# Two more groups of an attention and mixer kernel computed together with 7 block products instead of 8, and the attention of the last pairs placed earlier

## Chip, core and metric

One core of one Trainium2 chip runs the whole program. The time is device microseconds of one execution; runs of the same kernel agree within a few tenths of a per cent. Engines: PE (TensorE, matrix products), PEld (its weight loads), DVE (VectorE), ACT (ScalarE), POOL (GpSimd), SP (SyncE, which issues most transfers).

## What is computed

Batch 8, 8 heads, 576 rows, head width 64. Attention within chunks of 64 rows, then a low-rank mixing along the sequence, then a two-layer network on each row:

```python
scores = scale * np.matmul(q_c, k_c.transpose(0, 1, 2, 4, 3))   # 64 x 64 a chunk
attn = np.exp(scores - max); attn = attn / (sum + 1e-09)
x = np.matmul(attn, v_c)                        # to (8, 576, 512)
u = x + (xt @ U @ V).transpose(0, 2, 1)         # U: 576 x 32, V: 32 x 576
ch = np.maximum(u @ w_ch1, 0.0) @ w_ch2         # 512 -> 2048 -> 512
return u + ch
```

## The kernel before

**Tiles.** Two batches make a pair (pr 0 to 3) of 1152 rows, nine tiles of 128 rows (t 0 to 8). Three tiles are a group (pr, g). The network's 2048 inner columns are 16 blocks f of 128.

**Products in three parts.** Each float32 operand is split into a high part, rounded to fp32r, and a low part, the rest (ACT casts the high part, DVE or POOL subtracts it from the whole). A product is high x high, high x low and low x high.

**A plain block** (pr, g, f) is `hidden` (L1140): 12 products of 384 columns (4 of 128 inputs x 3 parts), relu on ACT (`relu_high`, tile hh) and its low part on DVE (`relu_low`, hl), and `project_out` (L1167): 3 tiles x 3 products of 512 columns. The second half of block f runs after the first half of block f+1, so its relu has time. Eight groups run like this: (0,0) to (2,1).

**A joint group** (`joint`, L1483) takes two groups at once, before ((2,2),(3,0)) and ((3,1),(3,2)). The products with w_ch1 of both groups are 2 x 2 blocks in which 7 block products take the place of 8, with sums of the operands (Strassen and Winograd's form). `combos` (L1348) makes the sums of the weights once (`wsum` on POOL and DVE, `wput` to DRAM, array wc); `Combos` (L1427) makes those of the inputs (`csum` on POOL, tiles us; `csplit`, high on ACT, low on DVE or POOL). A joint group has four chunks of four f. In a chunk the steps follow the list STEPS: A1 to A7 and B1 to B7 are block products, 6 products of 384 columns each, 84 in all, on the banks x, c and y of A and of B; Ga0 to Gb5 are the second layer, 6 products of 512 columns each, 72 in all. Several block products add to one bank, and the bank is copied by ACT (`snap`, L1505, tiles s1, s5, u2, u3) between two of them, so that the later product has to wait for the copy. DVE adds the copies, takes the low parts of relu and adds the output to the residual (xr) after each Gb.

Each block product reads a combined weight block of 128 KB from wc into one of 11 places (`issue`, kind w), splits it (`split_w`: ACT casts, POOL or DVE subtracts, 5 steps ahead), and is issued again 11 products later.

**Attention beside it.** Pair 0 runs first, in a planned opening part of about 100 us in which the weights are converted too. Tiles of pairs 1 to 3 come two at a time, in visits (`VISITS` and `visit`, L1599 to L1628). At a visit PE makes the scores of two tiles (sc) and the values (av) of the two tiles of the visit before; DVE takes the maximum and subtracts (8 steps), ACT takes exp (ex), DVE scales the values (x). In between, q and k come through a DRAM copy in another layout (`permute`) and are transposed on DVE (`turn`, L950); ex is summed and transposed on DVE (`turn_ex`) and goes to DRAM and back (`put_ex`, `get_ex`: exs, eT); v is loaded by POOL (`load_v`, vn). Then x is split (xh, xl), projected onto U (`project`, bank y), spilled (xd), fetched again, mixed (`Mix`: bank u, added to x), transposed on DVE, stored (ud) and sent through DRAM (xs, uf) to get features onto partitions.

**What sets the order.** Everything after the opening stands in an agenda: `at(key, s, ...)` puts work at tick s, counted in quarter blocks on PE (a block has 4 ticks, a joint chunk 32). A table TUNE shifts each key by some ticks and names the queue or engine of each transfer or subtraction (S, P, A). The kernel is issued in that order, each engine takes its instructions in order, and there is no other scheduler. All tiles of attention share nine slots of 2 KB a partition (tag slot); all banks of products come from eight.

Of the kernel before, what the change touches and what calls it, by code (L numbers as in the profile page):

```python
# [231 lines left out]
def kernel(  # L232
# [1396 lines left out]
    for i, (s, now) in enumerate(chain):  # L1629
# [10 lines left out]
        for z, a in enumerate(prev):  # L1640
# [4 lines left out]
            if a.pr > 1:  # L1645
                at("spill " + a.n, s + 2 + z, a.spill)
# [117 lines left out]
```

## Time and profile before

| | us |
|---|---|
| median of 3 runs (all) | 920.66 (917.64, 920.66, 922.95) |
| profiled execution, own time | 916.5 |
| its span, first to last instruction | 914.7 |
| PE busy | 893.9 (98%) |
| DVE busy | 527.5 (58%) |
| ACT busy | 294.0 (32%) |
| POOL busy | 245.7 (27%) |
| share of PE in the chain that ended last | 80% |

A product is pipelined: the next one starts before it ends, so the time of one (338 ns for 384 columns) is longer than the step from one to the next, and a busy PE is not yet PE at its pace. The pace is read from stretches in which nothing waits. An idle engine costs nothing as long as PE doesn't wait for it.

### The profile page before, as it was taken

Reading aid. Unit: us, or ns where it says so; the run is one execution under the profiler, and the core shown is the slowest. Engines: PE = TensorE matmul, PEld = TensorE weight load, DVE = VectorE, ACT = ScalarE, POOL = GpSimd, SP = SyncE. Lnnn points to the kernel's source line nnn. Section 1 sums busy time; section 2 is a strip of 40 time slices with the busy share of each in tenths; the row PEclk is TensorE's granted clock in tenths of the full one; section 3 lists DMA queues with packets and bytes.
Section 4 is the critical chain, followed back from the end, with each engine's and each line's share of the span. In section 5 each row is a group of like instructions: output and inputs, shape, how many; then the busy total and the mean of one; then the engine's idle time right before and its main releaser. Section 6 shows DMA issues by size and latency. Waiting matters only on the chain.

```text
span 914.7 us, 17206 instructions
## 1 busy us (share of the span) xinstructions
PE 893.9 (98%) x6500; PEld 789.5 (86%) x6500; DVE 527.5 (58%) x1022; ACT 294.0 (32%) x602; POOL 245.7 (27%) x363
## 2 busy tenths in 40 slices
PE   6899999999999999999999999999999999999998
PEld 5578989888889889888888888898889889988996
DVE  4799995566544437556356646555745547534433
ACT  5576761122211112122112212212544326423430
POOL 4300001031020022232303212377643346323320
PEclk9999999999999999999999999999999999999999
DMA  9994695677557546667868677588554542522201
GB/s 183 195 323 138 157 231 107 134 166 186 92 129 156 97 109 136 162 164 136 199 147 198 154 182 183 149 213 276 167 195 119 150 146 58 196 64 64 81 18 69
DMA packets 298882, 137.91 MB, mean 151 GB/s; under 512 B 197424, under 2 KB 278224, under 8 KB 298800
## 3 DMA queue, kind: packets, MB, share of 16 engines
q1 hardware_dynamic: 200224, 109.29, 44.6%
q10 hardware_dynamic: 92640, 14.09, 9.2%
q0 software_dynamic: 5936, 13.43, 5.6%
q8 instruction: 51, 0.84, 0.4%
q14 instruction: 31, 0.25, 0.1%
HBM read 97.17 MB, written 53.74 MB: 165 GB/s over the span
## 4 chain that ended last, share of the span: by engine, by line
PE 80%; DVE 6%; DMA 6%; issue 2%; SPq 2%; POOL 2%; ACT 1%; ACTq 0%; DVEq 0%; POOLq 0%
PE o L1179 24%; PE h L1151 24%; PE o L1553 15%; DMA qkv<-in_q_dram 2%; PE sc L970 2%; SPq L284 1%; PE av L1028 1%; PE x_3B L1578 1%; PE x_0B L1578 1%; PE x_2B L1578 1%; DVE wraw L323 1%; PE x_1B L1578 1%; PE x_3A L1578 1%; PE x_2A L1578 1%; DVE wroom L326 1%
## 5 line engine op out<-in xcount | busy, mean ns | idle before, releaser
L1151 PE MATMUL h<-uth,w 128*128 128x384 f32 x1024 | 282.2, 338 | 0.4 <-DVE ex L985 0.4
L1179 PE MATMUL o<-w,hh 128*128 128x512 f32 x768 | 242.7, 397 | 0.1
L1151 PEld LDWEIGHTS h<-uth,w 128*128 128x128 f32 x1024 | 187.5, 188 | 6.9 <-issue 1.2
L1164 DVE SCALAR_TENSOR_TENSOR hl<-h,hh 128x384 fp32r<-128x384 f32 x128 | 70.5, 552 | 179.8 <-ACT hh L1159 179.5
L1151 PE MATMUL h<-utl,w 128*128 128x384 f32 x512 | 173.0, 338 | 0.0
L1159 ACT ACTIVATE hh<-h 128x384 fp32r<-128x384 f32 x128 | 62.7, 490 | 325.1 <-PE h L1151 317.1
L1179 PEld LDWEIGHTS o<-w,hh 128*128 128x128 f32 x768 | 141.7, 188 | 24.9 <-ACT hh L1159 0.7
L1179 PE MATMUL o<-w,hl 128*128 128x512 f32 x384 | 151.9, 396 | 1.2 <-DVE hl L1164 1.2
L284 POOL DMA_DIRECT2D vn<-in_v_dram x96 | 58.9, 628 | 232.7 <-issue 104.7
L1151 PEld LDWEIGHTS h<-utl,w 128*128 128x128 f32 x512 | 96.2, 188 | 5.1 <-issue 0.2
L1179 PEld LDWEIGHTS o<-w,hl 128*128 128x128 f32 x384 | 72.2, 188 | 19.7 <-DVE hl L1164 2.7
L1421 POOL TENSOR_TENSOR w<-w,w 128x256 fp32r<-128x256 f32 x65 | 49.5, 776 | 79.8 <-ACT w L1420 78.7
L1563 DVE TENSOR_TENSOR xr<-o,xr 128x512 f32<-128x512 f32 x48 | 32.9, 690 | 57.8 <-PE o L1553 57.6
L1420 ACT CAST w<-w 128x256 fp32r<-128x256 f32 x112 | 41.5, 408 | 24.2 <-DMA w<-wc 16.3
L1056 POOL TENSOR_TENSOR xl<-x,xh 128x512 fp32r<-128x512 f32 x8 | 10.3, 1289 | 137.7 <-ACT xh L1052 137.7
L1421 POOL TENSOR_TENSOR w<-w 128x256 fp32r<-128x256 f32 x35 | 26.5, 762 | 54.2 <-ACT w L1420 51.7
L993 ACT ACTIVATE ex<-ex 128x512 f32<-128x512 f32 x27 | 17.1, 633 | 66.4 <-DVE ex L985 52.4
L984 DVE TENSOR_REDUCE mx<-sc 128x4 f32<-128x256 f32 x54 | 22.5, 416 | 15.9 <-PE sc L970 15.9
L985 DVE TENSOR_TENSOR ex<-sc,mx 128x256 f32<-128x256 f32 x54 | 22.9, 424 | 2.3
L950 DVE STREAM_TRANSPOSE qn<-qn 128x512 f32<-128x512 f32 x27 | 18.8, 697 | 6.1 <-DMA qn<-qblocks 5.1
L313 ACT ACTIVATE wroom<-wraw 128x1024 f32<-128x1024 f32 (+1 forms) x19 | 19.0, 1001 | 5.5 <-issue 4.1
L1028 PE MATMUL av<-vn,eT 64*64 64x64 f32 x864 | 18.3, 221 | 2.3 <-DVE hl L1164 1.2
(345 smaller groups left out, 1428.3 us busy)
## 6 DMA issues: line engine op xcount, KB each, us to landing
wraw<-in_moe_w_ch_dram SPq DMA_DIRECT2D x32, 512.0 KB, 6.2
w<-wc SPq DMA_DIRECT2D x105, 128.0 KB, 2.3
xs<-xb SPq DMA_DIRECT2D x108, 64.0 KB, 2.2
uf<-xs SPq DMA_DIRECT2D x26, 256.0 KB, 3.2
qn<-qblocks SPq DMA_DIRECT2D x24, 256.0 KB, 3.7
kn<-kblocks SPq DMA_DIRECT2D x24, 256.0 KB, 4.2
vn<-in_v_dram POOLq DMA_DIRECT2D x96, 64.0 KB, 3.3
exs<-ex SPq DMA_DIRECT2D x96, 64.0 KB, 2.3
```

Source lines behind the costliest of these rows:

```text
L284: {"S": nc.sync, "P": nc.gpsimd, "A": nc.scalar}[way].dma_start(dst, src)
L985: nc.vector.tensor_sub(self.ex[:, e].rearrange("p b h k -> p h b k"), self.sc[e].rearrange("p (h b k) -> p h b k", b=2, k=TB), mx[:, e].un ...
L1028: nc.tensor.matmul(ps[e][cs, (z * HP + hp) * C : (z * HP + hp + 1) * C], lhsT=self.eT[rows, hp, 2 * c : 2 * c + 2, :].rearrange("p a i -> ...
L1151: nc.tensor.matmul(ps[:, :GN], lhsT=w[:, z, cc], rhs=u[:, cc, :], start=(n == 0), stop=(n == 3 * NCC - 1))
L1159: nc.scalar.activation(hh, ps[:, :GN], AF.Relu)
L1164: nc.vector.scalar_tensor_tensor(hl, ps[:, :GN], 0.0, hh, op0=ALU.max, op1=ALU.subtract)
L1179: nc.tensor.matmul(acc[j], lhsT=h[:, js], rhs=w2[f][:, z], start=(first and i == 0), stop=(final and i == 2),)
L1420: nc.scalar.copy(h, l.bitcast(F32))
L1421: side("wlo", n).tensor_sub(l, l.bitcast(F32), h)
L1553: nc.tensor.matmul(acc[j], lhsT=u[:, q, js], rhs=w2[f][:, p], start=(z == "A" and e == 0 and n == 0), stop=(z == "B" and e == 1 and n == 2),)
L1563: nc.vector.tensor_add(xs[j], acc[j], xs[j])
L1578: nc.tensor.matmul(ps, lhsT=w[wz][:, cc], rhs=u[uz][:, cc], start=(k in (1, 2, 5) and cc == 0 and m == 0), stop=(cc == 1 and m == 2), skip ...
```

## The change

A third joint group ((2,0),(2,1)) is put ahead of the two, so the joint part begins after (1,2), at tick 384 instead of 512. The plain blocks of (2,0) and (2,1) go. Attention of pairs 2 and 3 is placed at earlier ticks (pair 2 every 20 ticks, where it was 28 and more); since three tiles of pair 3 would come too late for that, four visits lie inside the first joint group. Tiles 6 to 8 of pair 1 are spilled and fetched as well, the mixes of pair 2 store their result for the residual, and the order table is new: nearly all of its shifts and many of its queues differ, of which a few lines stand here. Line numbers after the table are 35 higher.

```diff
-        "perm 3.0.3": "P", "perm 3.1.0": "A", "perm 3.1.2": "S", "perm 3.1.3": "A",
+        "perm 3.1.0": "P", "perm 3.1.2": "S", "perm 3.1.3": "A", "perm 3.1.4": "S", "put": "S",
-    JOINED = 8 * NF * 4
+    JOINED = 6 * NF * 4
-    JOINT = [((2, 2), (3, 0)), ((3, 1), (3, 2))]
+    JOINT = [((2, 0), (2, 1)), ((2, 2), (3, 0)), ((3, 1), (3, 2))]
     def free(f):
-        return ("hidden", 2, 1, f) in done and ("sum", f // 2) in done
+        return ("hidden", 1, 2, f) in done and ("sum", f // 2) in done
     VISITS = [
         (94, 1, 0), (114, 1, 2), (138, 1, 4), (158, 1, 6), (198, 1, 8),
-        (221.5, 2, 0), (262, 2, 2), (290, 2, 4), (318, 2, 6), (346, 2, 8),
-        (366, 3, 0), (394, 3, 2), (420, 3, 4), (446, 3, 6), (480, 3, 8),
+        (221.5, 2, 0), (242, 2, 2), (262, 2, 4), (282, 2, 6), (302, 2, 8),
+        (322, 3, 0), (344, 3, 2), (404, 3, 4), (428, 3, 6), (450, 3, 8),
     ]
-    chain.append((510, []))
+    chain.append((470, []))
-            if a.pr > 1:
+            if a.pr > 1 or a.t > 5:
                 at("spill " + a.n, s + 2 + z, a.spill)
-            s1 = s + 2 if after - s < 30 else s + 20
+            s1 = s + 2 if after - s < 30 or s == 344 else s + 20
-    for (pr, e), s in {(2, 0): 140, (2, 1): 196, (3, 0): 290, (3, 1): 340}.items():
+    for (pr, e), s in {(2, 0): 140, (2, 1): 184, (3, 0): 236, (3, 1): 330}.items():
+            at(f"fetch 1.{t}", PAIR + NF * 4 + 4 + 8 * (t - 6), lambda t=t: Mix(1, t).fetch())
-    for t in range(6):
-        at(f"fetch 2.{t}", (345, 408)[t > 2] + 3 * (t % 3), lambda t=t: Mix(2, t).fetch())
-        plan_mix(2, t, (350, 413)[t > 2] + 3 * (t % 3))
     MIXES = {
-        (2, 6): 392, (2, 7): 395, (2, 8): 398,
-        (3, 0): 462, (3, 1): 465, (3, 2): 468, (3, 3): 560,
+        (2, 0): 294, (2, 1): 297, (2, 2): 300, (2, 3): 332,
+        (2, 4): 335, (2, 5): 338, (2, 6): 410, (2, 7): 413, (2, 8): 416,
+        (3, 0): 438, (3, 1): 441, (3, 2): 444, (3, 3): 560,
-    for pr, g in ((0, 2), (1, 0), (1, 1), (1, 2), (2, 0), (2, 1)):
+    for pr, g in ((0, 2), (1, 0), (1, 1), (1, 2)):
         for f in range(NF):
```

How the order moves at three places. First PE in the second chunk of the first joint group, from the second-layer step Ga0 (tile o_1_0) on, in the kernel before:

```order
L1553 MATMUL o_1_0_7749<-w_1128,hh_1A 128x512 x2
L1553 MATMUL o_1_0_7749<-w_1128,hl_1A 128x512
L1553 MATMUL o_1_0_7749<-w_1160,hh_1A 128x512 x2
L1553 MATMUL o_1_0_7749<-w_1160,hl_1A 128x512
L1578 MATMUL x_1B<-w_1396,w_1306 128x384
L1578 MATMUL x_1B<-w_1454,w_1306 128x384
L1578 MATMUL x_1B<-w_1396,w_1353 128x384
```

and in the change:

```order
L1588 MATMUL o_1_0_6536<-w_1160,hh_1A 128x512 x2
L1588 MATMUL o_1_0_6536<-w_1160,hl_1A 128x512
L1005 MATMUL sc<-kn_6_6257,qn_6_6256 64x64 x16
L1005 MATMUL sc<-kn_7_6411,qn_7_6410 64x64 x16
L1063 MATMUL av<-vn_4_6330,eT_4_6364 64x64 x16
L1063 MATMUL av<-vn_5_6350,eT_5_6464 64x64 x16
L1613 MATMUL x_1B<-w_1396,w_1306 128x384
L1613 MATMUL x_1B<-w_1454,w_1306 128x384
L1613 MATMUL x_1B<-w_1396,w_1353 128x384
```

A visit (scores of tiles 3_6 and 3_7, values of 3_4 and 3_5) now stands between Ga0 and the block product B7 on bank x of B. As before, Ga1 and then B4, on the same bank, follow B7.

Second ACT at the same place: hh is relu, u_0_1B the copy of bank x_1B, ex an exp, xh a split of x, the CASTs of w are weight blocks. Before:

```order
L1519 ACTIVATE hh_1B<-y_1B 128x384
L1420 CAST w_1607<-w_1607 128x256
L1519 ACTIVATE hh_1B<-c_1B 128x384
L1507 COPY u_0_1B<-x_1B 128x384
L1420 CAST w_1649<-w_1649 128x256
L1519 ACTIVATE hh_1B<-u_0_1B 128x384
```

In the change:

```order
L319 DMA w_1259<-wc_5523 128x256
L1554 ACTIVATE hh_1B<-c_1B 128x384
L1028 ACTIVATE ex_6_6579<-ex_6_6579 128x512
L1028 ACTIVATE ex_7_6583<-ex_7_6583 128x512
L1542 COPY u_0_1B<-x_1B 128x384
L1455 CAST w_1661<-w_1661 128x256
L1087 CAST xh_4_6652<-x_4_6627 128x512
L1554 ACTIVATE hh_1B<-u_0_1B 128x384
```

Both exps of the visit now stand ahead of the copy of x_1B.

Third DVE at the end of the last plain group, where the inputs' sums are split for the first joint group (w_1160 is the low part for the products A2 and B2, bank y; w_951 that for A1). Before:

```order
L1164 SCALAR_TENSOR_TENSOR hl_1_15_7231<-h_1_15_7216,hh_1_15_7229 128x384
L1473 TENSOR_TENSOR w_1082<-us_2_7233,w_1021 128x4x2x32
L1473 TENSOR_TENSOR w_1160<-uf_8_7154,w_1128 128x4x2x32
L1473 TENSOR_TENSOR w_1259<-us_2_7233,w_1219 128x4x2x32
L1473 TENSOR_TENSOR w_1353<-us_2_7233,w_1306 128x4x2x32
L1473 TENSOR_TENSOR w_1454<-us_2_7233,w_1396 128x4x2x32
L1040 TENSOR_TENSOR x_8_7273<-av,sm_8_6937 128x256 x2
L1473 TENSOR_TENSOR w_1160<-uf_7_7147,w_1128 128x4x2x32
```

In the change:

```order
L1508 TENSOR_TENSOR w_1353<-us_1_5817,w_1306 128x4x2x32
L1508 TENSOR_TENSOR w_1160<-uf_2_5753,w_1128 128x4x2x32
L1199 SCALAR_TENSOR_TENSOR hl_2_15_5844<-h_2_15_5829,hh_2_15_5842 128x384
L1508 TENSOR_TENSOR w_1454<-us_1_5817,w_1396 128x4x2x32
L1508 TENSOR_TENSOR w_951<-uf_2_5753,w_614 128x4x2x32
L1508 TENSOR_TENSOR w_1082<-us_2_5863,w_1021 128x4x2x32
L1508 TENSOR_TENSOR w_1259<-us_2_5863,w_1219 128x4x2x32
```

The last split for bank y stood after the last block's low part of relu (hl_1_15), four other splits and a visit's scaling (x_8); it now stands ahead of that low part (hl_2_15), and no visit's steps are near.

## Rows read from the trace of the kernel before

**Rows 1.** The page: busy us (share) xinstructions; the span in 40 slices, tenths.

```profile
PE 893.9 (98%) x6500; PEld 789.5 (86%) x6500; DVE 527.5 (58%) x1022; ACT 294.0 (32%) x602; POOL 245.7 (27%) x363
PE   6899999999999999999999999999999999999998
PEclk9999999999999999999999999999999999999999
```

**Rows 2.** The chain that ended last, in order of time: start us, us, what.

```profile
340.26 2.11 PE h L1151 x12
342.38 2.09 PE o L1179 x9
865.76 13.94 PE o L1553 x60
```

**Rows 3.** Two windows: us, busy us (xinstructions) of each engine, clock, DMA share, GB/s.

```profile
340.26:352.89 12.63, 12.63 (x65) 11.44 (x64) 6.64 (x14) 2.50 (x5) 6.32 (x10) 1.00 0.68 140
834.41:865.76 31.35, 31.35 (x157) 28.20 (x157) 12.53 (x21) 10.93 (x28) 8.06 (x12) 1.00 0.16 47
```

**Rows 4.** Waits of PE, 100 to 914 us: us in total, times, longest us.

```profile
PE y_0A L1578 <- ACT w L1472: 1.3, 1, 1.3
PE av L1028 <- DVE hl L1164: 1.2, 1, 1.2
PE av L1028 <- DMA eT<-exs: 1.0, 2, 0.6
PE o L1179 <- DVE hl L1164: 0.9, 1, 0.9
PE h L1151 <- DVE ex L985: 0.4, 1, 0.4
PE y_0A L1578 <- DVE w L1473: 0.2, 1, 0.2
```

**Rows 5.** Timeline, one visit: start us, us, engine line op tiles [idle before <-releaser].

```profile
576.46 1.16 PE L970 MATMUL sc<-kn,qn 64*64 64x64 f32 x64
578.63 0.73 PE L1179 MATMUL o<-w,hh 128*128 128x512 f32 x2
580.20 0.63 ACT L993 ACTIVATE ex<-ex 128x512 f32<-128x512 f32 x1 [4.53 <-DVE ex L985]
580.99 0.63 ACT L993 ACTIVATE ex<-ex 128x512 f32<-128x512 f32 x1 [0.16 <-DVE ex L985]
```

**Rows 6.** Lines L1473 and L1507: count, duration ns min/median/max, first and last start.

```profile
L1473 DVE TENSOR_TENSOR w<-us,w x23: 407/650/982, 644.2 to 784.3; 128x256 fp32r<-128x256 f32 x23
L1473 DVE TENSOR_TENSOR w<-uf,w x18: 407/414/956, 648.0 to 785.2; 128x256 fp32r<-128x256 f32 x18
L1507 ACT COPY u_1B<-x_1B x4: 470/479/480, 702.2 to 832.0; 128x384 f32<-128x384 f32 x4
```

**Rows 7.** Two more windows, columns as in rows 3.

```profile
100.00:125.00 25.00, 25.00 (x127) 22.53 (x126) 24.37 (x30) 18.05 (x24) 0.00 (x0) 1.00 0.81 196
600.00:625.00 25.00, 23.80 (x206) 21.18 (x205) 15.36 (x32) 4.48 (x10) 14.34 (x21) 1.00 0.84 221
```

**Rows 8.** Timeline of PE at the start of the joint part.

```profile
658.95 0.41 PE L1578 MATMUL y_0A<-w 128*128 128x384 f32 x1 [1.30 <-ACT w L1472]
659.52 0.62 PE L1578 MATMUL y_0A<-w,w 128*128 128x384 f32 x2 [0.16 <-DVE w L1473]
```

**Rows 9.** The page's transfers (KB, us to landing); POOL's groups (busy us, mean ns).

```profile
w<-wc SPq DMA_DIRECT2D x105, 128.0 KB, 2.3
vn<-in_v_dram POOLq DMA_DIRECT2D x96, 64.0 KB, 3.3
L284 POOL DMA_DIRECT2D vn<-in_v_dram x96 | 58.9, 628 | 232.7 <-issue 104.7 <-DMA xs<-xb 38.8 <-DVE utl L1138 29.7
L1421 POOL TENSOR_TENSOR w<-w,w 128x256 fp32r<-128x256 f32 x65 | 49.5, 776 | 79.8 <-ACT w L1420 78.7 <-PE x_1B L1578 1.0
```

**Rows 10.** Timeline of SP's issues, 648 to 655 us.

```profile
649.33 3.46 SPq L284 DMA_DIRECT2D w<-wc  x6
```

439 rows, old and new, of the table TUNE are left out of this document.

## Prediction

> **What bounds the kernel now.** I began with the page: how busy each engine is and the course over the span [rows 1]. TensorE (PE) is busy 98% of 914.7 us at the full granted clock, VectorE (DVE) 58%, GpSimd (POOL) 27%. Since the end of a pipelined product is modelled, that share alone proves nothing, so I took the pace from the chain that ended last [rows 2] and from two clean windows [rows 3]. Twelve 384-wide products take 2.11 us and nine 512-wide ones 2.09; three blocks (a block is one f of one group of three tiles) take 12.63 us, 4.21 each, with no idle time on PE. A joint chunk of 84 narrow and 72 wide products takes 31.35 us, also without idle time. In the first window DVE is busy 6.64 of 12.63 us and in the second 12.53 of 31.35. Next come PE's own waits from 100 us on [rows 4]: they sum to 5.0 us out of 815. So PE's stream of products sets the end; all else matters only where PE is made to wait. The time before 100 us stays: on PE the two orders read alike until about there.
>
> The sum is made against the profiled execution: span 914.7, own time 916.5, which is 4.2 under the median of 920.66 (runs 917.64 to 922.95). I carry the difference over to the median.
>
> **The products.** Groups (2,0) and (2,1) cost 32 blocks, 32 x 4.21 = 134.7 us, and become four joint chunks, 4 x 31.35 = 125.4: **9.3 us less** [rows 3]. The count gives a little less: 384 narrow products become 336, the 288 wide ones stay, and 48 x 2.11/12 is 8.4 [rows 2]. The chunk also shows narrow products at a slightly better pace, (31.35 - 72 x 13.94/60)/84 = 0.174 us against 0.176, so I take **-9.0**, ends -8.4 and -9.3. The Trainium skill, "TensorE: Matmul & The Clock Gate", section "Back-to-back issue gap", gives N/2.4 + 2.5 ns a product at the full clock, 162.5 ns for 384 columns; by that estimate the term would be -7.8 and my sum below -4.9. The trace's 0.174 to 0.176 decides.
>
> **What is added off PE** is hidden unless PE waits for it. The orders count DVE 1024 to 1071 instructions, ACT 666 to 774, POOL 368 to 456, SP 692 to 751. In it are 56 more weight blocks (each a 128 KB load landing in 2.3 us [rows 9], an ACT cast, and a subtraction of 0.78 us on POOL [rows 9] or a shorter one on DVE), 18 more additions of output, 21 more splits and 12 more sums of the operands. With 84 product steps in hand this costs nothing by itself; if its cover goes, it is the third rival.
>
> **Where PE can be made to wait anew.** Before, no attention ran beside a joint group but the last mixes. Now three visits (scores of two tiles, values of the two before) and a fourth for values lie inside the first joint group. A joint chunk leaves DVE 31.35 - 12.53 = 18.8 us [rows 3]. The second chunk gets, by the order, six input transposes, eight softmax steps, four scalings, two tiles' row sums and transposes of ex, a split and eleven steps of mixing: about 20.5 us by their lengths (0.4 to 0.7 us each). DVE then works some 33 of about 36 us. It can be that full without harm: from 100 to 125 us it is busy 24.37 of 25 and PE loses nothing [rows 7]. But joint steps read DVE and ACT results sooner than plain blocks do.
>
> - *Second chunk, the step after the visit.* A visit of the trace [rows 5]: scores start at 576.46; PE is back at its products at 578.63 (2.17 later); ACT starts the two exps at 580.20 and 580.99, the second ends at 581.62 (5.16 later). Now ACT has both exps ahead of the copy of x_1B (shown in the order above), and PE's last product on that bank, B4, must wait for the copy. From the visit's start PE has 2.17, then B7 6 x 0.174 and Ga1 6 x 0.232: B4 is wanted at 4.61. The copy ends at 5.16 + 0.48 [rows 6] + 0.1 for the signals, about 5.7. Wait **1.1 us**, plus what DVE is late with the softmax; I take +1.5, ends 0 and 3.0. The projection of tile 3_5 then needs a split that stands behind nine DVE steps: +0.5, ends 0 and 1.0.
> - *First chunk.* On POOL the four transfers of vn_3_2 stand behind two weight subtractions: 2 x 0.78 + 4 x 0.63 to issue + 3.3 to land = 7.4 us [rows 9], where PE has B7, Ga1, B4, Gb0, Gb1 and the scores left, about 7.3. +0.6, ends 0 and 1.8. The split for tile 3_3 is as tight: +0.3, ends 0 and 0.6.
> - *Third chunk.* SP has 43 issues there and 49 in the second (before: 24 and 29), up to 0.58 us each [rows 10]; the values' eT may land late: +0.5, ends 0 and 1.5, by the waits on eT of before, 1.0 us over two visits [rows 4].
> - *Earlier visits* come about every 25 us where it was 33 to 40. The waits at values were 1.2 + 1.0 us [rows 4]; +0.5, ends -1.0 and 2.2.
> - *Start of the joint part.* PE waited 1.3 + 0.2 us for y_0A [rows 4, 8]: the last split for that product stood on DVE behind five others and a visit's scaling. Now it stands before the last block's split (order above), and no visit is near: **-1.0**, ends -1.5 and +1.5.
>
> Sum: -9.0 + 1.5 + 0.5 + 0.6 + 0.3 + 0.5 + 0.5 - 1.0 = **-6.1 us**: span 908.6, own time 910.4, median **914.6**. All lower ends give -11.8, all upper ones +3.2; they won't come together.
>
> **Rivals.**
> 1. *The new waits don't come* (the order leaves room everywhere). Then -9.0 - 1.0 = -10.0: **910.7**. For it: DVE at 97% cost PE nothing [rows 7]. Against: the B4 wait follows from lengths alone.
> 2. *The waits pile up.* DVE steps that read two operands from SBUF stretch while POOL works: one form of L1473 has a median of 0.414 us and a maximum of 0.956, the other, made beside POOL's sums, a median of 0.650 [rows 6]. POOL gets more work, and the order puts 14 such DVE steps into the first two chunks. At 0.24 to 0.54 us more each (0.650 and 0.956 less 0.41), DVE falls 3.4 to 7.6 us behind, and each of three visits makes PE wait 2 us more: -6.1 + 6 = -0.1, **920.6**, no change. The Trainium skill, "GPSIMD Engine Reference", section "1. Specifications", says that POOL shares its SBUF interfaces with VectorE and contends with DVE instructions of two SBUF inputs; by that rule, which the spread just named agrees with, this rival would be the outcome. Against it: most of DVE's added steps read PSUM or one operand, and my lengths already contain a mean of it.
> 3. *Slower: weight blocks come late behind SP.* In three chunks SP carries 138 issues (before 81), and weight loads stand behind transfers that wait for DVE or for each other's landing. ACT casts in order, so a late load holds back the copies that PE needs, step after step. If each of the 42 products waits 0.35 us, that is 14.7: -6.1 + 14.7 = +8.6, **929.3**. It decides from about 0.25 us a product (10.5 us, +4.4). For it: the densest SP stretch of before, 600 to 625 us with DMA 84% busy, is one where PE lost 1.2 [rows 4, 7]. Against: no product of the joint groups of before waits for a load, and loads are issued eleven blocks ahead.
>
> That the change doesn't do what it says is no rival: the order on PE shows 48 narrow products fewer.
>
> **How the numbers follow.** About 0.5% (4.6 us) is what a measurement of this kernel can tell from no change. Forecast (-8.5 to -4.6): 0.45. Rival 1: 0.17. Rival 2 (-4.6 to +4.6): 0.25. Rival 3: 0.13. So faster 0.62, same 0.25, slower 0.13. The range goes from a little below rival 1, 910.0, to 922.0, past rival 2's centre; left out are rival 3, the upper part of rival 2 and a little below: about 2 in 10.
>
> **What would show it.** Right: the four chunks of the new joint group at 31.3 us plus projections, mixes and visits; PE's waits in the first joint group 2 to 5 us in all, the longest at x_1B of the second chunk behind an ACT copy; about no wait at y_0A; the last two joint groups as before. Wrong: waits of PE's weight products on casts of w in most steps (rival 3); waits of 2 us and more at each visit with DVE over 95% in the first two chunks (rival 2); no wait over 0.5 us there (rival 1); or new idle time before 450 us, which I put at half a microsecond.

## The result and the profile after

The change is **slower** by 1.4%: median 933.43 us (932.18 to 934.07, 4 runs) against 921.14 (917.64 to 922.95, 4 runs), ratio 1.0136 with a 95% interval of 1.0104 to 1.0169. Forecast were 914.6 us and a range of 910 to 922. Unaltered once more beside later experiments it gave 934.53, ratio 1.0164 (1.0142 to 1.0186). The profiled execution took 933.8 us, its span is 932.0 (before 914.7, forecast 908.6). The page after, its first part and its line of the clock, answers to [rows 1]:

```profile
PE 895.8 (96%) x6452; PEld 785.1 (84%) x6452; DVE 560.6 (60%) x1069; ACT 327.5 (35%) x705; POOL 313.5 (34%) x451
PEclk9999999999999999999999999999999999999999
```

PE carries out 48 products fewer and yet is busy 2 us longer; its weight loads, PEld, fell by 4.4. The reason is in the rows below. PE's waits after, from 100 us on (in total, times, longest), to be read against [rows 4]:

```profile
PE y L1105 <- DVE xl L1091: 4.0, 5, 1.9
PE y L1104 <- ACT xh L1087: 2.6, 2, 1.7
PE sc L1005 <- DVE x L1226: 2.0, 1, 2.0
PE x_1B L1613 <- ACT u_1B L1542: 1.9, 1, 1.9
PE x_3B L1613 <- ACT u_3B L1542: 1.5, 2, 1.3
PE x_2A L1613 <- ACT u_2A L1542: 1.4, 2, 0.7
PE av L1063 <- DMA eT<-exs: 1.4, 2, 0.9
PE h L1186 <- DVE ex L1020: 1.2, 2, 0.8
PE x_0A L1613 <- ACT w L1507: 1.1, 1, 1.1
```

With eight smaller groups they sum to 20.5 us in 28 waits, before to 5.0 in 7. By stretch, in windows of before (columns as in [rows 3]):

```profile
100.00:350.00 250.00, 248.36 (x1810) 221.84 (x1809) 148.24 (x286) 66.57 (x116) 32.32 (x50) 1.00 0.64 141
350.00:525.00 175.00, 174.00 (x1501) 155.04 (x1500) 100.88 (x219) 35.17 (x67) 41.41 (x60) 1.00 0.71 164
525.00:675.00 150.00, 147.34 (x1083) 131.93 (x1082) 86.01 (x170) 40.73 (x94) 71.24 (x94) 1.00 0.71 200
```

and of the change, with a chunk of the last joint group and three windows of 25 us behind:

```profile
100.00:350.00 250.00, 246.15 (x1912) 218.58 (x1911) 156.02 (x306) 69.53 (x119) 42.15 (x62) 1.00 0.71 155
350.00:525.00 175.00, 165.51 (x1315) 145.50 (x1314) 98.74 (x205) 36.34 (x78) 90.31 (x119) 0.98 0.86 217
525.00:675.00 150.00, 142.78 (x1029) 123.32 (x1028) 103.71 (x192) 62.05 (x160) 79.13 (x111) 0.99 0.64 175
865.46:896.82 31.36, 31.36 (x158) 28.20 (x156) 12.17 (x21) 11.35 (x29) 8.84 (x12) 1.00 0.20 59
350.00:375.00 25.00, 22.82 (x220) 19.84 (x219) 15.11 (x34) 4.89 (x9) 7.85 (x12) 0.93 0.98 232
425.00:450.00 25.00, 23.09 (x192) 19.87 (x192) 13.13 (x27) 3.53 (x7) 9.01 (x12) 0.93 0.67 173
575.00:600.00 25.00, 22.85 (x215) 19.10 (x214) 21.40 (x44) 8.13 (x20) 12.10 (x18) 0.93 0.75 207
```

Length less PE's busy time is idle time. From 100 to 350 us it rose from 1.6 to 3.9, from 350 to 525 (plain blocks, visits of pairs 2 and 3) from 1.0 to 9.5, from 525 to 675 (the new joint group) from 2.7 to 7.2: **15.3 us more**. The chunk of the last joint group is as it was, 31.36 us, and 48 products are gone, so I count the products' 9.0 as given; in the new joint group no chunk is free of waits. And in three windows the granted clock is 0.93 where it was 1.00: 25 x 0.07 = 1.75 us of PE's work in each, **5.2 us**. That makes -9.0 + 15.3 + 5.2 = +11.5 of the 17.3 us of span, in this execution. The 5.2 need not be a cost by themselves: of the four executions one had a mean granted clock of 1.00, and its span was 931.3 us, 0.7 less than this one. Another part hides in the busy time: a product of PE is drawn with a modelled end, so a stop is longer than its idle time. At the wait of 1.87 us shown further down, the starts lie 2.27 apart where the pace is 0.23, so 2.04 are lost: 0.17 more. For 21 more stops that is 3.6 us; 2.2 are left unexplained. The Trainium skill, "Perfetto Trace Analysis", section "Tensor Engine Instruction (MATMUL, LD_WEIGHTS)", says that PE's end times are estimated from the size of the instruction; here PE's busy time rose by 2.0 with less work.

Where the time is lost can be listed by place. "Lost" is the time from start to start of PE's products over their pace [rows 2] (for the 64-wide ones of a visit 0.018 us, from [rows 5]), summed over the place, the slow clock behind it included; it is good to a few tenths. "Again" is the second execution, of the unaltered change.

| us | what PE waits for | lost | again |
|---|---|---|---|
| 363 to 370 | scores of 2_4, 2_5: additions of output on DVE behind a late k; then slow clock (not again) | 4.3 | 1.3 |
| 389 to 395 | values: low part of relu on DVE (again: eT) | 0.8 | 1.1 |
| 427 to 438 | projection of 2_6: relu and xh on ACT behind a load of k; slow clock | 4.0 | 6.2 |
| 472 to 477 | a visit's scores and values | 1.2 | 1.5 |
| 480 to 490 | projections of 3_0, 3_1: xh, xl behind the next visit's steps; again: slow clock | 4.8 | 6.5 |
| 531 to 536 | product A7: splits of its inputs | 2.3 | 2.2 |
| 555 to 563 | projections of 3_2, 3_3: xl | 1.2 | 1.8 |
| 579 to 593 | B4 behind the copy of x_1B; slow clock (not again) | 4.4 | 4.3 |
| 609 to 618 | copies of x_2A behind an exp | 2.5 | 2.5 |
| 653 to 661 | copies of x_3B behind splits for the next joint group | 2.2 | 2.2 |

Ten places, 28 us in one execution and 30 in the other. In the kernel before the same windows lose some 4 us, half of that at the start of its joint part (659 us).

Two of them in the timeline. First PE, ACT and ACT's queue of transfers (ACTq) at 426 to 436 us; "qn" and "kn" are q and k of tile 3_1, whose load ACT issues:

```profile
431.71 0.34 PE L1186 MATMUL h<-uth,w 128*128 128x384 f32 x1
433.72 0.49 PE L1104 MATMUL y<-xh,ust 128*128 128x512 f32 x1 [1.68 <-ACT xh L1087]
435.58 1.05 PE L1214 MATMUL o<-w,hh 128*128 128x512 f32 x2
...
425.83 0.61 ACTq L319 DMA_DIRECT2D qn<-qblocks  x1
432.02 0.55 ACTq L319 DMA_DIRECT2D kn<-kblocks  x1
432.67 0.49 ACT L1194 ACTIVATE hh<-h 128x384 fp32r<-128x384 f32 x1 [6.37 <-PE h L1186]
433.06 1.13 ACT L1087 CAST xh<-x 128x512 fp32r<-128x512 f32 x2
```

The load of k is issued at 432.0 instead of 426.4. The chain of waits names the cause: the slot it goes to was an xb tile, whose transfer xs, issued at 426.3, had not landed.

```profile
426.29 5.64 DMA xs<-xb
```

ACT takes its work in order, so relu and xh stand behind the load, and PE has nothing for 1.7 us and then only one product for another 0.2. What follows stands in windows of 1 us: the granted clock falls to half, 1.2 GHz, between 435 and 436 us, some 1.6 us after PE came back, and PE is busy while it stays there.

```profile
432.00:433.00 1.00, 0.05 (x1) 0.00 (x0) 0.00 (x0) 0.33 (x1) 0.00 (x0) 1.00 0.01 2
435.00:436.00 1.00, 1.00 (x4) 0.75 (x3) 1.00 (x4) 0.00 (x0) 0.92 (x1) 0.67 0.11 24
436.00:437.00 1.00, 1.00 (x4) 0.80 (x3) 0.67 (x2) 0.00 (x0) 0.37 (x1) 0.50 0.67 136
439.00:440.00 1.00, 1.00 (x7) 1.00 (x6) 0.00 (x0) 0.00 (x0) 0.00 (x0) 1.00 0.79 139
```

Second the place that the prediction named, the second chunk behind the visit of 3_6 and 3_7, on PE, ACT, DVE and POOL:

```profile
583.16 0.40 PE L1588 MATMUL o<-w,hl_1A 128*128 128x512 f32 x1
585.43 2.23 PE L1613 MATMUL x_1B<-w,w 128*128 128x384 f32 x6 [1.87 <-ACT u_1B L1542]
...
583.65 1.36 ACT L1028 ACTIVATE ex<-ex 128x512 f32<-128x512 f32 x2 [3.05 <-DVE ex L1020]
584.92 0.46 ACT L1542 COPY u_1B<-x_1B 128x384 f32<-128x384 f32 x1
...
586.83 1.43 DVE L1034 TENSOR_SCALAR sm<-sm 128x8 f32<-128x8 f32 x1
...
586.92 1.30 POOL L1091 TENSOR_TENSOR xl<-x,xh 128x512 fp32r<-128x512 f32 x1
```

The copy stands behind both exps, as forecast; 1.87 us for 1.1 to 1.5, and then the six products of B4 take 2.23 us at the slow clock. In the second execution the wait is there again, and the clock of this stretch stays at 1.00:

```profile
PE x_1B L1613 <- ACT u_1B L1542: 2.0, 1, 2.0
...
575.00:600.00 25.00, 21.87 (x217) 18.05 (x216) 21.43 (x43) 9.36 (x23) 13.16 (x19) 1.00 0.76 202
```

The place loses as much (4.3 for 4.4 us): PE's idle time is 3.1 us for 2.2, with waits of 0.6 us for the visit's values and for xl. So what the slow clock takes, other waits can take in its stead.

### The profile page after: what moved, and what is told of

Its sections match the earlier page's. It is cut to its first block, busy times and chain, and to the rows that moved or that the text cites. A ratio compares the mean times of both kernels' runs of the same rounds, so it can differ in the third digit from the quotient of the medians.

```text
span 932.0 us, 17562 instructions
## 1 busy us (share of the span) xinstructions
PE 895.8 (96%) x6452; PEld 785.1 (84%) x6452; DVE 560.6 (60%) x1069; ACT 327.5 (35%) x705; POOL 313.5 (34%) x451
## 4 chain that ended last, share of the span: by engine, by line
PE 78%; DVE 7%; DMA 6%; SPq 3%; ACT 2%; issue 2%; POOL 2%; ACTq 0%; DVEq 0%; POOLq 0%
PE o L1588 19%; PE o L1214 19%; PE h L1186 18%; DMA qkv<-in_q_dram 2%; SPq L319 2%; PE x_0A L1613 1%; PE x_2B L1613 1%; PE x_3A L1613 1%; PE x_3B L1613 1%; PE sc L1005 1%; PE x_1B L1613 1%; PE x_0B L1613 1%; DMA kn<-kblocks 1%; PE x_2A L1613 1%; PE x_1A L1613 1%
## 5 line engine op out<-in xcount | busy, mean ns | idle before, releaser
L1186 PE MATMUL h<-uth,w 128*128 128x384 f32 x768 | 211.6, 339 | 1.2 <-DVE ex L1020 1.2
L1214 PE MATMUL o<-w,hh 128*128 128x512 f32 x576 | 183.3, 399 | 0.5 <-ACT hh L1194 0.5
L1186 PEld LDWEIGHTS h<-uth,w 128*128 128x128 f32 x768 | 140.9, 188 | 6.0 <-issue 1.4
L1186 PE MATMUL h<-utl,w 128*128 128x384 f32 x384 | 130.0, 338 | 0.0
L1214 PEld LDWEIGHTS o<-w,hh 128*128 128x128 f32 x576 | 106.9, 189 | 19.7 <-ACT hh L1194 1.4
L1214 PE MATMUL o<-w,hl 128*128 128x512 f32 x288 | 114.9, 399 | 1.1 <-DVE hl L1199 1.1
L1456 POOL TENSOR_TENSOR w<-w,w 128x256 fp32r<-128x256 f32 x100 | 75.0, 761 | 118.4 <-ACT w L1455 117.3
L1186 PEld LDWEIGHTS h<-utl,w 128*128 128x128 f32 x384 | 72.3, 188 | 4.1 <-DVE utl L1173 0.4
L1588 PE MATMUL o<-w,hh_1B 128*128 128x512 f32 x72 | 23.1, 402 | 0.0
L1588 PE MATMUL o<-w,hh_2A 128*128 128x512 f32 x72 | 22.6, 395 | 0.0
```

The source lines that it names most:

```text
L1186: nc.tensor.matmul(ps[:, :GN], lhsT=w[:, z, cc], rhs=u[:, cc, :], start=(n == 0), stop=(n == 3 * NCC - 1))
L1214: nc.tensor.matmul(acc[j], lhsT=h[:, js], rhs=w2[f][:, z], start=(first and i == 0), stop=(final and i == 2),)
L1456: side("wlo", n).tensor_sub(l, l.bitcast(F32), h)
L1588: nc.tensor.matmul(acc[j], lhsT=u[:, q, js], rhs=w2[f][:, p], start=(z == "A" and e == 0 and n == 0), stop=(z == "B" and e == 1 and n == 2),)
```

## Experiments

Two theories to begin with. **A**: each place is one instruction that stands ahead of what PE needs, on an engine that works in order; mend the place and its time is saved. **B**: the transfers as a whole run short (the DMA engines are busy 0.86 from 350 to 525 us, before 0.71), so a mended place shows up elsewhere. The kernel before, measured beside each of them, took 918.5 to 920.3 us.

**One place each.** The numbers are shifts in the order table (quarter blocks) and queues; of each line of the table only the entries that change are shown.

```diff
-        "qk 3_1": "A"
+        "qk 3_1": "S"
```

> The changed kernel with one edit: the q and k of tile 3_1 are loaded by SP instead of ACT. In the changed kernel's trace the load of k stands on ACT from 425.8 to 432.0 us, waiting until a transfer of the input transposes has left the slot, and the relu behind it is 4 us late; PE waits 1.9 and 0.6 us for the projection of tile 2_6 at 431.7 and then runs at half the clock for some 3 us. Theory A (single instructions that stand ahead on an engine that works in order): all of it goes, 4.2 us less than the changed kernel, 929.2 for 933.4; no wait at that projection, no fall of the clock near 435. Theory B (the transfers are too slow as a whole, 0.86 of the DMA engines' time from 400 to 525 us): SP is held instead, what stands behind it comes late, and PE waits nearly as long a little later: 1 us less or none.

930.58 us, ratio 1.0107 (1.0076 to 1.0138). Theory A at its place: no wait, no idle time, full clock.

```profile
425.00:450.00 25.00, 25.00 (x214) 22.50 (x213) 15.94 (x36) 5.40 (x11) 13.32 (x17) 1.00 0.85 224
```

Of 4.2 us forecast 2.9 arrived, which the intervals hardly tell from none: 470 to 490 us lost 2.0 more than in the change, for there the granted clock was 0.91 in this execution and 1.00 in that of the change, at the same idle time (4.5 us).

```diff
-        "project 3_0": -0.75, "project 3_1": -1.0
+        "project 3_0": 3, "project 3_1": 5
```

> The changed kernel with one edit: the projections of tiles 3_0 and 3_1 stand about four and six quarter blocks later on PE. In the changed kernel PE waits there 1.2 + 1.6 + 2.2 us (482 to 488 us) for the high and low parts, which stand on DVE behind eight softmax steps, four scalings and row sums. Theory A: 4.6 us less, 928.8, no wait at these projections. Theory B: 1.5 us less at most, the wait turns up at the next step that needs a transfer.

932.12 us, ratio 1.0116 (1.0079 to 1.0153). The projections wait no more, but the next product of a plain block does, for the low part of relu, which stands on DVE behind the same visit (1.2 us), and the joint part starts with 2.1 us of waits for the splits:

```profile
PE x_0A L1613 <- ACT w L1507: 1.5, 1, 1.5
PE o L1214 <- DVE hl L1199: 1.2, 1, 1.2
PE x_0A L1613 <- DVE w L1508: 0.6, 1, 0.6
```

```diff
-        "visit 3_4": -0.25,
+        "visit 3_4": -0.25, "visit 3_6": 1,
```

> The changed kernel with one edit: the visit of tiles 3_6 and 3_7 stands behind the block product B7 instead of ahead of it, so that ACT copies bank x of B ahead of the two exps. In the changed kernel PE waits 1.9 us for that copy at 585.4 and then runs 3 us at half the clock. Theory A, which is also the prediction's account of this place: 4.0 us less, 929.4; no wait at x_1B of the second chunk, no fall of the clock. Theory B: 1 us less at most.

934.65 us, ratio 1.0143 (1.01 to 1.0186): nothing. The wait at x_1B is gone, and the projections of 3_4 and 3_5 a few microseconds later wait instead:

```profile
PE y L1105 <- DVE xl L1091: 1.9, 1, 1.9
PE y L1105 <- DVE sm L1034: 1.3, 1, 1.3
```

The four edits together (with `"load 2_5"` from 1.5 to -1.5):

> The three edits together and a fourth: the q and k of tile 2_5 are loaded three quarter blocks earlier (they land at 362.8 and 364.6 in the changed kernel, DVE waits for them ahead of the additions of output that the scores of tiles 2_4 and 2_5 wait for: 2.0 us of PE's time at 363.7 and 2.5 at half the clock behind it). Theory A: the savings add up, 4.2 + 4.6 + 4.0 + 4.3 = 17 us less, 916.4, about 5 us faster than before; granted clock 1.00 throughout. Theory B: 5 us less at most, 928, and new waits elsewhere.

934.16 us, ratio 1.0139 (1.0095 to 1.0183). At the places named the waits went as A has it (425 to 450 us: none), in the median nothing did; the executions spread from 929.58, the profiled one, to 936.79. So A in its simple form fell: a place is not paid by itself. B had the sum right, and the next four runs went after it.

**Less and more to transfer.** Leave out the copies of pair 3:

```diff
-            dma(
+            pr == 3 or dma(
                 "perm",
```

> The changed kernel with the 16 copies of q and k of pair 3 (288 KB each, read and written in small pieces) left out; pair 3 reads those of pair 2 instead, so its output is of other data. The order on PE, DVE and POOL's arithmetic stays. Against the plain pace PE loses 17.0 us from 350 to 525 us in the changed kernel and 3.2 in the kernel before; the DMA engines are busy 0.87 and 0.71 of that stretch. Theory B (the transfers are the supply that runs short; an instruction that waits for one or for one of the nine slots holds its engine, and another place pays when this one is mended): the share falls to about 0.7, PE's loss there to about 6 us, the time by 11 to about 922. Theory A (the places themselves, each with its order): the loss stays above 13 us, the time at 930 or more.

931.96 us, ratio 1.015 (1.0126 to 1.0173). The share fell as meant, PE's idle time did not (9.49 to 8.36):

```profile
350.00:525.00 175.00, 166.64 (x1323) 147.13 (x1322) 98.95 (x208) 36.85 (x81) 89.99 (x118) 0.98 0.74 195
```

Only the place at 363 us went, where a load of k was late. From 475 to 500 us the share fell from 0.99 to 0.66, and PE is busy 21.01 us for 20.79: that place does not hang on busy DMA engines.

The four edits, and the copies of the second batch of pair 3 from tick 272 instead of 330:

> The kernel of the four edits, and the eight copies of q and k for the second batch of pair 3 placed 58 quarter blocks earlier (from about 450 to 500 us to about 375 to 430 us, where the DMA engines are busy 0.67 to 0.84 instead of 0.98). Theory B: the loss that the four edits moved to 500 to 525 us (6.0 us) and to 550 to 600 us (8.9) shrinks by half, 6 to 8 us less than with the four edits, 927 for 934. Theory A: no more than 2 us of difference.

933.17 us, ratio 1.0159 (1.0128 to 1.019), no gain. The idle time from 500 to 525 us went, as B has it (2.5 us with the four edits, now 0.1), that from 550 to 600 us hardly (5.2, now 4.7), and from 350 to 525 us 6.2 stay of 6.6. A late eT at 188 us (3.7 us, in that execution) took the rest back.

Eight copies more in the kernel before:

```diff
+    for k in range(8):
+        at(f"extra {k}", 297 + 12 * k, lambda k=k: extra(k))
```

> The kernel before with eight more copies of 288 KB from DRAM to DRAM in the same small pieces, which nobody reads, spread by POOL over about 400 to 515 us, where its POOL has little to do. Theory B: the share of the DMA engines there rises from 0.73 to about 0.93 and PE loses 5 to 10 us more there, 926 to 931. Theory A (the order, not the supply): 1 us more at most, 922.

919.23 us (10 runs), ratio 1.0000 (0.9974 to 1.0026). The share from 400 to 525 us rose to 0.84, less than meant, PE's idle time there did not:

```profile
400.00:525.00 125.00, 124.54 (x1023) 110.73 (x1022) 67.26 (x147) 25.20 (x48) 39.80 (x55) 1.00 0.84 188
```

Theory B fell as the main cause: on the mean of the stretch the change's own 0.86 is hardly more than that. That a single late transfer can hold an engine, as at 427 us, is not touched by it.

**Theory C**, DVE too full inside the joint group: transposes left out there.

```diff
-                nc.vector.transpose(z, z)
+                self.pr == 3 and self.t > 3 or nc.vector.transpose(z, z)
```

> The changed kernel with the transposes of q, k and ex on DVE left out for tiles 3_4 to 3_8 (15 of about 0.68 us, 10 us of DVE, nearly all in the first joint group), so the output is of other data. PE loses 13.4 us there (525 to 675 us) against the plain pace. Theory C (inside the joint group DVE is the supply: 40 of 50 us busy from 550 to 600): the loss falls to 6 to 8 us, the time by 6 to 927; 350 to 525 us stays. Theories A and B: less than 3 us gained there, 931 or more.

931.54 us, ratio 1.0146 (1.0122 to 1.0169): the idle time of 525 to 675 us went from 7.2 to 8.3, not down. The steps left out are not those that PE waits behind.

**The attention alone.** The kernel before with the visits of the change and their order, joint groups as before (`VISITS`, the copies' ticks and the attention's keys of the order table):

> The kernel before (two joint groups, joint part from tick 512) with the attention of the change alone: its visits, its order of all attention steps and their queues, its copies of q and k; the sums of the weights, the joint groups and the mixes of pairs 2 and 3 as before. So the products are those of before, and from 404 to 470 the visits lie among plain blocks. Theory D (each visit is a stretch of some 13 us that DVE and ACT need one after the other; visits every 25 us put more of PE's steps into such stretches): PE loses 10 to 14 us more than the kernel before, 929 to 933. Theory J (it is the neighbours that the third joint group brings: sums of weights and of inputs, copies of banks): 3 us more at most, 922.

925.33 us (7 runs), ratio 1.0081 (1.0053 to 1.011): 7 us, between theories D and J. Idle 2.6, 4.0 and 4.0 us in the three stretches, 10.5 in all, for 5.3 before and 20.6 in the change:

```profile
100.00:350.00 250.00, 247.43 (x1919) 219.94 (x1918) 157.11 (x308) 69.25 (x119) 42.76 (x62) 1.00 0.72 156
350.00:525.00 175.00, 171.03 (x1360) 152.41 (x1359) 88.76 (x187) 32.28 (x62) 43.56 (x65) 0.99 0.70 161
525.00:675.00 150.00, 146.01 (x1074) 130.61 (x1073) 83.35 (x165) 36.43 (x83) 67.00 (x87) 1.00 0.62 173
```

The places at 363 and 392 us are there, those at 427 to 438 not, of 480 to 490 a third. The denser visits cost some 7 us by themselves; the rest comes with the third joint group. By which part of it was tried for the sums of the weights alone.

**Which neighbours.** Without the arithmetic of the weights' sums, without their transfers, without both:

```diff
-                side("wadd", f).tensor_add(b, a[:, 0:DM], a[:, DM:])
+                i > 1 or side("wadd", f).tensor_add(b, a[:, 0:DM], a[:, DM:])
...
-                dma(
+                i > 1 or dma(
                     "wput",
```

The four subtractions behind the additions are left out in the same way.

> The changed kernel without the arithmetic of the weights' sums from the third of eight on (two additions and four subtractions each, on POOL and DVE, from about 440 to 520 us); the transfers stay, of stale data. PE loses 11.0 us from 425 to 525 us there. If POOL's and DVE's work of the sums is what the attention collides with: 5 us less or more, 928. If it is the attention alone: less than 2 us, 932.

> The changed kernel without the transfers of the weights' sums to DRAM from the third of eight on (all chunks read the first one's blocks); the arithmetic stays. If these transfers on SP and in the DMA engines are what the attention's transfers wait behind: 5 us less, 928. If not: less than 2 us, 932.

> Both left out. Theory J: nearly all of the loss from 425 to 525 us that the attention alone did not show (11.0 against 2.6 us) goes, 925. Theory D (the attention's own stretch on DVE and ACT): 3 us at most, 930.

931.12, 930.88 and 929.16 us; ratios 1.0117 (1.0057 to 1.0178), 1.0127 (1.0067 to 1.0187), 1.0102 (1.0048 to 1.0156). PE's busy time from 425 to 525 us, 93.39 in the change, was 95.36, 93.39 and 94.94: the arithmetic is worth at most 2 us of idle time, the transfers none. The second execution of the unaltered change has 91.50 there, so two executions differ by as much, and the profiled ones of e13 and e15 are the fastest of their four. With these intervals no total is told apart from that of the change, 933.43. The places stayed where they were. So theory J fell for the sums of the weights; which other neighbours matter (sums and splits of the inputs, copies of banks) is not shown.

**Lighter visits** in the joint group:

```diff
-            nc.vector.reduce_max(mx[:, e],
+            self.pr == 3 and self.t > 3 or nc.vector.reduce_max(mx[:, e],
```

> The changed kernel with DVE's maxima, row sums, reciprocals and transposes left out for tiles 3_4 to 3_8 (some 8 us of DVE a visit, in the first joint group), the subtraction, exp, scaling and all the rest kept. Theory D: PE's 13.4 us of loss from 525 to 675 us falls to about 5, the time by 7 to 8, 925 to 926. If it is the other engines (ACT's casts, POOL, transfers): 10 us or more stay, 931.

930.01 us, ratio 1.0111 (1.0045 to 1.0178). The waits for x_1B and for xl are gone, from 555 to 600 us little is lost, but others stand as before or grow:

```profile
PE x_2B L1613 <- DVE ex L1020: 1.7, 1, 1.7
PE x_3B L1613 <- ACT u_3B L1542: 1.5, 2, 1.3
PE x_0A L1613 <- ACT w L1507: 1.1, 1, 1.1
PE x_2A L1613 <- ACT u_2A L1542: 1.1, 2, 0.7
```

So DVE's steps at the visits hold the second chunk, as theory D has it (3.3 us by starts, of 8 forecast); A7 and x_3B are held by the order on ACT, x_2A and x_2B by an exp: DVE's subtraction ahead of it waits for a slot (4.7 us until xs has left, 2.6 in the change).

**Many places at once**, now with the steps that follow each place moved too: `qk 3_1` by SP, copies from 272, and (again only the entries that change)

```diff
-        "project 3_0": -0.75, "project 3_1": -1.0, "project 3_2": 0.5, "project 3_3": 3.0
+        "project 3_0": 3, "project 3_1": 5, "project 3_2": 2.5, "project 3_3": 4.5
-        "csplit 0.2.7": 10, "csplit 1.0.5": 1, "csplit 1.1.5": 1, "csplit 1.2.5": 0.5
+        "csplit 0.2.7": 8, "csplit 1.0.5": 3, "csplit 1.1.5": 3, "csplit 1.2.5": 3
```

once with the visit of 3_6 behind B7, the projections of 3_4 and 3_5 some three ticks later and the mixes of 3_0 to 3_2 2.5 ticks later (e10), once without all of these (e12):

> The changed kernel with the places mended together, each by its own step: k of 3_1 loaded by SP; copies of q and k of pair 3 earlier; projections of 3_0 to 3_5 two to six quarter blocks later (the mixes of 3_0 to 3_2 with them); the visit of 3_6 behind B7; the last split for A7 two quarter blocks earlier; the splits for A5 and B5 of the second joint group two later. Theory D: waits at 431 (4.0), 482 (3.3), 531 (2.2), 557 and 561 (1.1), 580 to 590 (3), 654 to 660 (2.2) go, 16 us less, 917 to 918. If half of it comes back at the steps that follow, as with the four edits: 925.

> The same without the move of the visit of 3_6 and of the projections of 3_4 and 3_5 (the wait at x_1B of the second chunk, 4.4 us with the clock behind it, stays). Theory D: 921 to 922; with half coming back: 928.

929.69 us, ratio 1.0129 (1.0098 to 1.016), and 928.11, 1.0104 (1.0082 to 1.0126): e10 above both of its forecasts, e12 where half comes back. e12 showed two more places: eT of 3_4, which ACT loads, held ACT at 560 us, and the visit of 3_8 waited for a slot. With those two and the load of 2_5:

```diff
-        "getex 3_4": "A", "load 2_5": 1.5
+        "getex 3_4": "S", "load 2_5": -1.5, "visit 3_8": 2
```

> The kernel of the spaced places without the visit's move (e12), with three more edits: q and k of 2_5 loaded three quarter blocks earlier, eT of 3_4 loaded by SP instead of ACT (ACT stood behind it and PE waited 2.4 us for the copy of x_1A at 560 us), the visit of 3_8 two quarter blocks later (DVE waited 2.7 us there for a slot). If each place pays for itself (theory A): 928.1 less 2.7, 1.5 and 2, 922. If half comes back: 925.

**926.12 us**, ratio 1.0066 (1.0048 to 1.0084). The unaltered change beside it:

> The changed kernel, unaltered, on the chip of e17: how far the places and their waits repeat from one execution to another. Expected: 932 to 934; each wait of over 0.5 us between 400 and 660 us within 0.3 us of the first profile, that at 187 us (a transfer) not.

934.53 us, 1.0164 (1.0142 to 1.0186). Eight edits of order took back 8 us, clear of both intervals; that is some two fifths of what the seven mended places had cost (21 and 23 us by the table, all but 389, 472 and 579). Those held by DVE and ACT repeat within 0.1 to 0.7 us between the two executions of the change (expected were 0.3); where a transfer decides they don't (363 us, and the load of k at 427 us: 3.8 us of waiting for 1.7). No version here beats the kernel before.

## Why the prediction was wrong

- **Bound by PE, products -9.0**: right as far as shown. 48 products are gone, and a chunk without waits is 31.36 us.
- **y_0A, -1.0**: right in kind: no wait for y_0A is left. But product A7 five steps on lost 2.3 us to the same splits, in every kernel of the change's own order; I looked at the first product of the joint group alone.
- **Second chunk, +1.5 for B4**: the place, the engine and the order were right, 1.87 us (the 0.1 us for signals had no row behind it; from the copy's end at 585.38 to B4's start 0.05 pass). What stands around it was missing: the place lost 4.4 us, with the slow clock in one execution and with waits for values and xl in the other.
- **The other terms of the joint group** (+0.6, +0.3, +0.5, +0.5): PE does not wait for vn, nor for eT in the third chunk; at the projections of 3_2 and 3_3 it waits 0.65 us, at those of 3_4 and 3_5 not at all in the first execution and 0.6 us in the second. Instead it waits for A7 (1.3 us), for copies of x_2A (1.4) and of x_3B (1.5), of which the sum has no term. The idle time from 525 to 675 us rose by 4.6 us; the terms were 3.4 in all, less 1.0.
- **"Earlier visits ... +0.5, ends -1.0 and 2.2"** is the step that failed. I sized it by the waits at values alone. The stretches from 100 to 525 us became idle for 10.7 us more and lost 3.5 to the clock; from 100 to 450 us, which the prediction named as a sign of being wrong, the idle time is 8.6 us for 2.1. The waits are mostly not at values but at scores and at projections, three of them behind loads and splits that I had not followed through the order: a load on ACT's queue that waits for a slot, xl behind the next visit's eight softmax steps. The attention alone (e11) showed some 7 us where I had half a microsecond; for the rest I had no term.
- **"84 product steps in hand"**: wrong as a cover. The work added fits DVE and ACT in sum (60% and 35% busy), but PE needs it at given places.
- **The clock**: [rows 1, 3] show it at 1.00 throughout, and I left it out of the sum. It fell behind three long stops, 5.2 us of PE's work in that execution; an execution at 1.00 was only 0.7 us shorter, so a term for it would not have mended the sum.
- **Rivals.** Rival 3 came near the time (929.3) by luck, with the wrong mechanism: no product waits for a load of weights, and e14 left transfers on that queue out for nothing. Rival 2 was the nearest in kind (waits at visits, behind DVE) and too small: three visits at 2 us where there were ten places at about 1 to 6. Its own sign did not come, DVE over 95% in the first two chunks: it is busy 52.4 of 68 us from 525 to 593. Its cause, POOL, is there in the rows of the sum steps: L1034 takes 0.17 us at its shortest and 1.43 at 586.8, until POOL's subtraction ends (586.92 + 1.30). The Trainium skill, "Trainium Architecture — The Big Picture", section "What this means for kernel authors", calls the port pair of VectorE and GpSimd an exclusive lock; these two rows agree. Of the 27 steps of L1034, 11 take over 0.3 us, and each of these ends within 0.04 us of the end of an operation on POOL; in the kernel before it is 7 of 27. What that costs PE is not shown: POOL's sums taken away (e13) gave back 2 us at most, and no run moved the subtractions of xl off POOL.
- Chances: slower had 0.13, with a single mechanism behind it. Ten places that each were tight by a microsecond deserved more than a term of half a microsecond and ends that "won't come together".

What stays open: why more than half of what the mended places cost comes back, and what in the third joint group makes 933.4 us of the 925.3 of the attention alone. The runs show the time arriving at the next step that waits behind the same visit (e3, e4) or at a fall of the clock (e1), not through the share of the transfers (e6, e8); it was not followed place by place.

## What to carry to other kernels

When work is moved beside a stream that never waits, sum the added waits place by place: for every product that needs another engine's result, what stands ahead of that result in its engine's order, and what that in turn waits for (a slot, a landing). Shares of busy time say nothing of it: with DVE at 60% and ACT at 35% PE waits 20.5 us, with 58% and 32% it waits 5.0. A transfer that waits for a slot belongs on a queue whose engine computes nothing that is needed soon (e1). And one mended place proves little: the wait goes to the step behind it. With the steps behind moved too, two fifths of the cost came back here.

## Not expected of the hardware

In the first profile the granted clock of PE fell to 0.50 behind three stops of 1.7 to 2.0 us (363.9, 432.0 and 583.6 us), about 1, 1.6 and 0.1 us after PE had resumed, and stayed there about 3 us. It is not the stop's length alone: two waits of 1.20 and 1.89 us at 484 and 488 us left it at 1.00 in this execution, and in the second one the same place brought the window of 475 to 500 us to 0.86:

```profile
475.00:500.00 25.00, 21.56 (x110) 18.15 (x100) 12.62 (x30) 4.72 (x11) 19.38 (x24) 0.86 0.99 236
```

And the wait at x_1B, 1.87 us in one and 2.0 in the other, had the fall behind it in the first execution alone. So whether a stop of two microseconds brings the clock down changes from one execution to the next. Where it does, PE loses 1.75 us more, but the time of the kernel need not be longer by as much.
